# Dynamic convolution and squared-ReLU network: band matrices in one VectorE op, and another order for the softmax pieces and the first loads

## The chip, the cores and the metric

The kernel runs on one core of one Trainium2 chip. The metric is the device time of one execution in microseconds. The kernel before took 760.06 us in the median of eight runs (758.33 to 762.07).

## What is computed

Two stages follow each other. The first is a dynamic convolution over a sequence: each token and each of 8 heads has its own 7 weights, which a softmax makes from `weight_gen`. The second is a feed-forward network with a squared ReLU.

```python
# x: 8 x 4096 x 192, weight_gen: 8 x 4096 x 8 x 7, float32
w = exp(weight_gen - max); w = w / (sum(w) + 1e-9)         # over the 7 taps
x_unf = x_pad[:, s + k, :]                                 # 6 zero rows ahead
out = einsum('bshk,bskhg->bshg', w, x_unf)                 # 24 channels a head
h = np.maximum(out.reshape(32768, 192) @ w_in, 0.0)        # w_in: 192 x 2048
return h * h @ w_out                                       # w_out: 2048 x 192
```

## The kernel before

The 32768 tokens are cut into 64 sub-blocks of 512 tokens, 8 to a batch. `BLOCKS` puts them into 33 blocks: two of one sub-block each, then 31 of two.

**Convolution.** For each sub-block TensorE multiplies pieces of x (tokens on the partitions, 32 channels as the stationary operand) with band matrices. A sub-block has five tiles of 128 tokens that start 104 tokens apart (`STEP`). Each tile gives 104 output columns, the last one 96. A band matrix is the softmax rows of a tile (`wr`, 64 values per token) times a mask that keeps 7 diagonals. `st_band` (L315) makes it on VectorE for one or more tiles in one op, into `bd`. The op is cut as `st_bands` (L474) says: tiles 0 and 1, tiles 2 and 3, tile 4. The first sub-block of a batch has tile 0 alone, because that tile starts at token 0. Where a softmax part ends with the sub-block, tile 4 starts at another place (`tile_start`, L258), and the band has other mask columns. `st_conv` (L372) is the matmuls and the copies of their result to `y` by ScalarE (L401).

**Network.** `st_unit` (L406), called a unit, is six matmuls of 512 columns into one of three PSUM tiles of the pool `ps_h`, which the convolution uses too. ScalarE evicts it with the ReLU into `t` (L424, five buffers). VectorE squares it into `g` (L427). A double block has 16 units, a single one 8. `st_mm2` (L437) is half of the second product for 256 tokens, a quarter of a double block. It runs one block later, into the only pair of output tiles (`ps_o`, one buffer). After the two halves ScalarE copies one of the pair (L461) and VectorE adds the other to it (L462, in `o_sum`). Then the pair is free for the next quarter.

**Order.** The order is written out by hand: the scheduler is set to manual, and each engine executes its instructions in the order in which the program issues them. In `steady`, M is a half of the second product for the block before, u a unit of this block, C the convolution of the next block:

```python
orders = {0: "uuuuuCuuu", 1: "MuMuuuMuuuMCu", 2: "MuuuuMuuuuMuuuuuuuMCu"}
steady = "MuMuuu" * 3 + "MuuuMCu"
```

Ahead of unit u of block j, `run_fill` (L622) issues what the table `fill` holds for (j, u): bands of the next block, exponentials, or a softmax piece (`soft`).

**Softmax.** Each batch is cut into parts (`PARTS`, else one part of 32 rows per partition). Batch 0 has four parts of 8 rows, batch 1 has 8, 8 and 16, batch 2 has 16 and 16. A part has 6 rows of halo and is worked on in pieces of 8 rows (a last piece has 6). A piece is an exponential on ScalarE (L194), and on VectorE a sum (L201), a reciprocal (L208) and the products (L216). Their places are in `TIMES`. The results of small parts go straight into the tiles `wr` by DMAs from SBUF to SBUF (`move_rows`, L491, alternating between the queues of SyncE and GpSimd). Those of large parts are stored in DRAM and read back (`wr_load`).

**Start.** The program loads the first part (s0), w_in and x, computes s0, casts w_in and x on ScalarE (L528, L291), makes the bands and the convolution of sub-block 0, then the exponential, bands and softmax that sub-blocks 1 to 3 need (L536 to L545). GpSimd's queue has the row moves, w_out (L549), a memset of `v_big` (L552) and the x loads of sub-blocks 2 and 3. All loads by GpSimd's queue convert from float32 to float16. The memset at L547 orders the w_out loads behind the cast of x for sub-block 1.

Of the kernel before, what the change touches and what calls it, by code (L numbers as in the profile page):

```python
# [9 lines left out]
def kernel(  # L10
# [25 lines left out]
    nc = tc.nc  # L36
# [10 lines left out]
    P = 128  # L47
# [75 lines left out]
    def cross_w_in(q):  # L123
        for r0, r1 in ((0, RT), (RT, 0)):
            nc.sync.dma_start(out=w_i[r0 : r0 + RT, q, 1], in_=w_i[r1 : r1 + RT, q, 0])
# [132 lines left out]
    def tile_start(j, i):  # L258

        t1 = (j % NBB + 1) * TB  # L260
        return TB - P if i == NT - 1 and t1 in ends(j // NBB) else starts[i]
# [52 lines left out]

    def st_band(j, tiles):  # L315

        if j not in bd_t:
            bd_t[j] = p_bd.tile([P, H * TB], f16, name="bd")
        i = tiles[0]
        lo, hi, n = bounds[i], bounds[tiles[-1] + 1], bounds[i + 1] - bounds[i]  # L320
        shift = 0 if i == 0 and j % NBB == 0 else lo - tile_start(j, i)
        shape = (P, HP * len(tiles), n // SL, 2 * SL)
        nc.vector.tensor_tensor(  # L323
            out=bd_t[j][:, H * lo : H * hi].rearrange(
                "p (g m c) -> p g m c", g=shape[1], c=2 * SL
            ),
            in0=wr_t[j][:, i : tiles[-1] + 1]
            .rearrange("p t g c -> p (t g) c")
            .unsqueeze(2)
            .broadcast_to(shape),  # L330
            in1=mask[:, shift : shift + n]
            .rearrange("p (m c) e -> p m (c e)", c=SL)
            .unsqueeze(1)
            .broadcast_to(shape),
            op=AluOp.mult,
        )
# [35 lines left out]
    def st_conv(j):  # L372

        n = BLOCKS[j][1]
        th = n * TB // 2
        per = 1024 // th
        y = p_y.tile([P, NK, TB], f16, name="y")
        y_t[j] = y
        yps = [
            ps_h.tile([P, 2 * TB], f32, name="yp", tag="h") for _ in range(-(-NK // per))  # L380
        ]
        for later, s, i, q, half, a, b, base in conv_pieces(j):
            lo, hi = bounds[i], bounds[i + 1]
            _, ha, hb, pre = quads[q]
            m, h = (32, hb) if later else (pre, ha)
            bd = bd_t[s][:, H * lo : H * hi].rearrange("p (g c e) -> p g e c", g=HP, e=2)
            p0 = RT * half + 32 * (q % 2)
            k = q // 2
            col = th * (k % per) - base
            nc.tensor.matmul(  # L390
                out=yps[k // per][p0 : p0 + m, col + a : col + b],
                lhsT=x_t[s][:, i, 32 * q : 32 * q + m],
                rhs=bd[:, h // 2, h % 2, a - lo : b - lo],
                start=True,
                stop=True,
                skip_group_check=True,
                tile_position=(0, p0),
            )
        for n, yp in enumerate(yps):
            k0, k1 = n * per, min((n + 1) * per, NK)  # L400
            nc.scalar.copy(  # L401
                out=y[:, k0:k1, 0:th],
                in_=yp[:, 0 : (k1 - k0) * th].rearrange("p (k c) -> p k c", c=th),
            )
# [66 lines left out]
            ],  # L471
        )

    def st_bands(j, part):  # L474

        groups = ((0,), (1,), (2, 3)) if j % NBB == 0 else ((0, 1), (2, 3))
        for tiles in (groups, ((NT - 1,),))[part]:
            st_band(j, tiles)

    with nc.allow_low_precision("fp16 matmul pipeline"), tc.manual_schedule():  # L480

# [42 lines left out]
        s0.total(0, s0.rh)  # L524
        s0.recip(0, s0.rh)
        s0.scale(0, s0.rh, nc.vector)
        for q in (0, 1):
            nc.scalar.copy(out=w_i[:, q, 0], in_=w_st[q])  # L528
        wr_load_sbuf(0, [s0], (0, 2, 1, 4, 3), (nc.sync, nc.gpsimd))
        wr_load_sbuf(1, [s0], range(NT), (nc.gpsimd,))  # L530
        for q in (0, 1):
            cross_w_in(q)
        x_cast(0, nc.scalar.copy)
        x_load_f32(1)
        s1.load(nc.sync)
        for i in (0, 2, 1, 3, 4):  # L536
            st_band(0, (i,))
        st_conv(0)
        s1.exp(0, s1.rh)
        st_bands(1, 0)  # L540
        st_bands(1, 1)
        x_cast(1, nc.vector.tensor_copy)
        s1.total(0, s1.rh)
        s1.recip(0, s1.rh)
        s1.scale(0, s1.rh, nc.vector)  # L545

        nc.gpsimd.memset(x_st[1][:, 0:1], 0.0)  # L547
        for q in range(4):
            load_w_out(q, 4)  # L549
        move_rows(s1)  # L550
        s2.load(nc.sync)
        nc.gpsimd.memset(v_big, 0.0)  # L552
        x_load(2)
        x_load(3)

# [7 lines left out]
        def at(j, u, kind, *args):  # L565
# [2 lines left out]
        PIECE = 8  # L568

        TIMES = {  # L570
            (0, 2): ((1, 7), (2, 1)),
            (0, 3): ((2, 15), (3, 1)),
            (1, 0): ((3, 15), (4, 1)),
            (1, 1): ((4, 15), (5, 1)),
            (1, 2): ((5, 9), (5, 15), (6, 1)),
            (2, 0): ((6, 15), (7, 1), (7, 9)),
            (2, 1): ((8, 1), (8, 15), (9, 1)),
            (3, 0): ((9, 9), (9, 15), (10, 9), (10, 15), (11, 1)),
        }

        EXP_AT = {1: 0, 7: 4, 9: 4, 15: 8}
        loads = {}
        for n, s in enumerate(parts[2:], 2):
            b, f = s.b, s.fb
            k = n - min(m for m, p in enumerate(parts) if p.b == b)
            times = TIMES.get((b, k)) or (
                (f - 6, 15), (f - 5, 15), (f - 4, 15), (f - 3, 9), (f - 3, 15)
            )
            pieces = [(lo, min(lo + PIECE, s.rh)) for lo in range(0, s.rh, PIECE)]
            for (j, u), (lo, hi) in zip(times, pieces, strict=True):  # L590
                at(j, EXP_AT[u], "exp", s, lo, hi)
                at(j, u, "soft", s, lo, hi)
            if n > 2:
                loads.setdefault(times[0][0] - 1, []).append(s)
        for j in range(1, NBLK - 1):
            a = BLOCKS[j + 1][0]
            when = (1, 9, 5, 9)
            if j == 1:
                when = (1, 1, 3, 3)
            elif j == 2:  # L600
                when = (5, 6, 8, 9)
            elif j in (3, 4, 5):
                when = (5, 7, 9, 11)
            elif j == 6:
                when = (9, 9, 11, 11)
            for u, args in zip(when, ((a, 0), (a, 1), (a + 1, 0), (a + 1, 1))):
                at(j, u, "band", *args)

        stored, waiting = set(), []

# [11 lines left out]
        def run_fill(j, u):  # L622
            for kind, *args in fill.get((j, u), ()):
                if kind == "band":
                    st_bands(*args)
                    continue
                s, lo, hi = args
                if kind == "exp":
                    s.exp(lo, hi)
                    continue  # L630
                s.total(lo, hi)
                s.recip(lo, hi)
                s.scale(lo, hi, nc.vector)
                if hi < s.rh:
                    continue
                if s.r == FIRST:
                    move_rows(s)
                    after = parts[parts.index(s) + 1]
                    if after.b == s.b and after.r > FIRST:
                        s.store(nc.sync)  # L640
                else:
                    s.store(nc.sync)
                    stored.add(s)
                    for w in [w for w in waiting if w[0] is s]:
                        waiting.remove(w)
                        load_rows(w[1])

        FCS = (range(NF // 2), range(NF // 2, NF))
        for j, (sub, n) in enumerate(BLOCKS):
            for s in loads.get(j, ()):  # L650
                s.load(nc.sync)
            if j + 2 < NBLK:
                load_rows(j + 2)
            u = m = 0
            for step in orders.get(j, steady):
                if step == "M":
                    qt, part = divmod(m, 2)
                    m += 1
                    if part == 0:
                        o = new_o(ps_o, None)  # L660
                    st_mm2(j - 1, qt, FCS[part], (0, 1), o)
                    if part == 1:
                        o_sum(j - 1, qt, (0, 1), o)
                        if qt % 2:
                            o_store(j - 1, qt - 1, range(4), nc.sync)
                elif step == "u":
                    run_fill(j, u)
                    st_unit(j, u)
                    u += 1
                elif j + 1 < NBLK:  # L670
                    st_conv(j + 1)
            if 0 < j < NBLK - 2:
                for k in range(BLOCKS[j + 2][0], sum(BLOCKS[j + 2])):
                    x_load(k)

# [46 lines left out]
```

The softmax here doesn't subtract the row's maximum and nothing guards it: scores larger than these inputs give would overflow.

## Time and profile before

| | before |
|---|---|
| median of eight runs, us | 760.06 |
| profiled execution, us | 761.96 |
| its span, us | 760.0 |
| mean granted TensorE clock | 0.991 |
| TensorE busy, us (matmuls) | 742.2 (15266) |
| VectorE busy, us (instructions) | 630.7 (1119) |
| ScalarE busy, us (instructions) | 623.6 (753) |
| band ops on VectorE (L323) | 201, 157.9 us |

All rows but the first are of one profiled execution, which is 1.9 us above the median. Its time is 2.0 us longer than its span, the time from the first instruction to the end of the last one. Busy time is the time in which an engine had an instruction in execution. In rows of groups, the numbers after the bar are busy time, the mean of one in ns, and the idle time of the engine just ahead of them with what ended it. In rows of waits the numbers are microseconds in total, how many times, and the longest. In rows of the timeline they are start and length in microseconds, and in brackets the idle time before. PE is TensorE, DVE VectorE, ACT ScalarE, POOL GpSimd, SP SyncE.

### The profile page before, as it was taken

Reading aid. Unit: us, or ns where it says so; the run is one execution under the profiler, and the core shown is the slowest. Engines: PE = TensorE matmul, PEld = TensorE weight load, DVE = VectorE, ACT = ScalarE, POOL = GpSimd, SP = SyncE. Lnnn points to the kernel's source line nnn. Section 1 sums busy time; section 2 is a strip of 40 time slices with the busy share of each in tenths; the row PEclk is TensorE's granted clock in tenths of the full one; section 3 lists DMA queues with packets and bytes.
Section 4 is the critical chain, followed back from the end, with each engine's and each line's share of the span. In section 5 each row is a group of like instructions: output and inputs, shape, how many; then the busy total and the mean of one; then the engine's idle time right before and its main releaser. Section 6 shows DMA issues by size and latency. Waiting matters only on the chain.

```text
span 760.0 us, 33723 instructions
## 1 busy us (share of the span) xinstructions
PE 742.2 (98%) x15266; PEld 560.1 (74%) x15266; DVE 630.7 (83%) x1119; ACT 623.6 (82%) x753; POOL 87.3 (11%) x126
## 2 busy tenths in 40 slices
PE   7899999999999999999999999999999999999998
PEld 4757877877787777777777777777777777777777
DVE  5888999898899988898888888888888887778853
ACT  3887889878888888888888888888888888888883
POOL 3522212011100110010100110001100011000000
PEclk8899999999999999999999999999999999999999
DMA  7844532546325544344445323454422454332311
GB/s 227 121 80 84 102 89 60 101 103 138 70 59 123 107 78 59 101 79 85 80 77 117 89 64 56 78 134 89 78 60 42 79 107 76 60 68 49 56 45 64
DMA packets 122395, 65.23 MB, mean 86 GB/s; under 512 B 83881, under 2 KB 118668, under 8 KB 121740
## 3 DMA queue, kind: packets, MB, share of 16 engines
q1 hardware_dynamic: 78012, 46.46, 21.4%
q0 software_dynamic: 44096, 16.53, 19.7%
q8 instruction: 119, 1.95, 1.0%
q14 instruction: 24, 0.20, 0.1%
q10 hardware_dynamic: 144, 0.10, 0.0%
HBM read 48.61 MB, written 28.70 MB: 102 GB/s over the span
## 4 chain that ended last, share of the span: by engine, by line
PE 86%; DVE 5%; issue 2%; DMA 1%; ACT 1%; POOL 0%; POOLq 0%; SPq 0%; DVEq 0%
PE o L447 42%; PE h L415 39%; PE yp L390 5%; DVE g L427 2%; DVE bd L323 2%; DMA xt<-in_x_dram 1%; DVE o_sb L462 1%; ACT o_sb L461 0%; DMA wr<-v_first 0%; ACT t L424 0%; DVE v_big L216 0%; DVE rcp L208 0%; DVE ssum L201 0%; POOL xt L277 0%; POOL xt L271 0%
## 5 line engine op out<-in xcount | busy, mean ns | idle before, releaser
L424 ACT ACTIVATE t<-h 128x1024 f16<-128x1024 f32 x512 | 496.9, 1027 | 71.2 <-PE h L415 69.5
L427 DVE TENSOR_TENSOR g<-t 128x1024 f16<-128x1024 f16 x512 | 336.3, 686 | 97.9 <-ACT t L424 95.8
L447 PEld LDWEIGHTS <-g 64*128 64x128 f16 x8192 | 351.1, 94 | 61.2 <-issue 8.9
L447 PE MATMUL o<-w_o,g 64*128 64x192 f16 x8192 | 384.2, 243 | 5.7 <-DVE o_sb L462 4.7
L415 PE MATMUL h<-y,w_i 64*128 64x512 f16 (+1 forms) x3168 | 380.3, 373 | 4.2 <-ACT t L424 2.7
L415 PEld LDWEIGHTS <-w_i 64*128 64x128 f16 x3168 | 164.0, 95 | 118.2 <-issue 6.5
L323 DVE TENSOR_TENSOR bd<-wr,mask 128x1664 f16<-128x1664 f16 (+2 forms) x201 | 157.9, 829 | 4.9 <-DMA wr<-v_first 4.9
L277 POOL DMA_DIRECT2D xt<-in_x_dram x62 | 51.3, 832 | 442.9 <-PE yp L390 420.0
L461 ACT COPY o_sb<-o 128x384 f32<-128x384 f32 x129 | 62.2, 482 | 33.5 <-PE o L447 33.5
L462 DVE TENSOR_TENSOR o_sb<-o,o_sb 128x384 f32<-128x384 f32 x129 | 71.1, 551 | 13.0 <-ACT o_sb L461 7.1
L401 ACT CAST y<-yp 128x1024 f16<-128x1024 f32 (+1 forms) x64 | 48.2, 803 | 15.9 <-PE yp L390 15.8
L390 PE MATMUL yp<-bd,xt 128*32 128x104 f16 (+8 forms) x3864 | 52.0, 209 | 3.1 <-ACT xt L291 1.8
L390 PEld LDWEIGHTS <-xt 128*32 128x32 f16 (+3 forms) x3864 | 46.2, 92 | 9.3 <-issue 6.0
L194 ACT ACTIVATE ex<-wg 128x448 f32<-128x448 f32 (+2 forms) x44 | 27.2, 618 | 6.5 <-DMA wg<-in_weight_gen_dram 6.5
L201 DVE TENSOR_REDUCE ssum<-ex 128x64 f32<-128x448 f32 (+2 forms) x44 | 26.1, 592 | 3.7 <-ACT ex L194 3.7
L216 DVE TENSOR_TENSOR v_big<-ex,rcp 128x112 f16<-128x112 f32 (+1 forms) x136 | 27.3, 263 | 1.2
L208 DVE RECIPROCAL rcp<-ssum 128x64 f32<-128x64 f32 (+2 forms) x44 | 23.7, 539 | 1.5
L307 POOL DMA_DIRECT2D wr<-v_first x31 | 16.8, 562 | 27.2 <-DVE v_first L216 27.2
L267 POOL DMA_DIRECT2D xt<-in_x_dram x7 | 3.8, 549 | 137.5 <-PE yp L390 137.5
L508 PE MATMUL wp<-warm 128*128 128x512 f16 x42 | 11.0, 430 | 1.3 <-DVE warm L500 1.3
L508 PEld LDWEIGHTS <-warm 128*128 128x128 f16 x42 | 4.5, 109 | 7.3 <-issue 2.4
L216 DVE TENSOR_TENSOR v_first<-ex,rcp 128x112 f16<-128x112 f32 (+1 forms) x48 | 9.1, 255 | 0.3
(17 smaller groups left out, 23.9 us busy)
## 6 DMA issues: line engine op xcount, KB each, us to landing
out_dram<-o_sb SPq DMA_DIRECT2D x63, 384.0 KB, 2.6
xt<-in_x_dram POOLq DMA_DIRECT2D x42, 240.0 KB, 5.9
wg<-in_weight_gen_dram SPq DMA_DIRECT2D x4, 1064.0 KB, 6.5
xt<-in_x_dram POOLq DMA_DIRECT2D x20, 192.0 KB, 6.3
wr<-vd SPq DMA_DIRECT2D x38, 80.0 KB, 5.0
vd<-v_big SPq DMA_DIRECT2D x5, 512.0 KB, 5.7
wg<-in_weight_gen_dram SPq DMA_DIRECT2D x6, 392.0 KB, 4.7
wg<-in_weight_gen_dram SPq DMA_DIRECT2D x3, 616.0 KB, 6.1
```

The source lines that it names most:

```text
L194: nc.scalar.activation(out=self.ex[:, lo:hi].rearrange("p r g k e -> p (r g) k e"), in_=self.wg[:, lo:hi].rearrange("p r (g e) k -> p (r g ...
L216: eng.tensor_tensor(out=bass.AP(tensor=v.tensor, offset=v.offset + lo * H * SL + lo % SL * 2 + g * SL * 2, ap=[list(v.ap[0]), [H * SL + 2, ...
L277: eng.dma_start(out=dst[:, first:last], in_=ap)
L323: nc.vector.tensor_tensor(out=bd_t[j][:, H * lo : H * hi].rearrange("p (g m c) -> p g m c", g=shape[1], c=2 * SL), in0=wr_t[j][:, i : tile ...
L390: nc.tensor.matmul(out=yps[k // per][p0 : p0 + m, col + a : col + b], lhsT=x_t[s][:, i, 32 * q : 32 * q + m], rhs=bd[:, h // 2, h % 2, a - ...
L401: nc.scalar.copy(out=y[:, k0:k1, 0:th], in_=yp[:, 0 : (k1 - k0) * th].rearrange("p (k c) -> p k c", c=th),)
L415: nc.tensor.matmul(out=h[:, half, jj * th : (jj + 1) * th], lhsT=w_in_chunk(u * per + jj, slot, half), rhs=y_t[j][r0 : r0 + RT, k, 0:th], ...
L424: nc.scalar.activation(out=t1, in_=h, func=ActF.Relu)
L427: nc.vector.tensor_tensor(out=g, in0=t1, in1=t1, op=AluOp.mult)
L447: nc.tensor.matmul(out=oo[:, cc * Dm : (cc + 1) * Dm], lhsT=g[r0 : r0 + RT, cc * P : (cc + 1) * P], rhs=w_o[r0 : r0 + RT, fc, :], start=(f ...
L461: nc.scalar.copy(out=o_sb, in_=o[0][:, c])
L462: nc.vector.tensor_tensor(out=o_sb, in0=o[1][:, c], in1=o_sb, op=AluOp.add)
```

## The change

It has four parts.

1. All five band tiles have the same width of 104 columns, the last one included, so that `bd` has 520 columns per head and not 512. `st_bands` makes one op of all five tiles. Tile 0 stays alone at the start of a batch, and tile 4 stays alone where a softmax part ends. The convolution reads the same columns as before.
2. The second softmax part, s1, is worked on within block 0: its exponential ahead of unit 4, the rest ahead of unit 5.
3. The softmax pieces get new places in `TIMES`. A place (j, 0) is the first unit of a block, with the exponential ahead of unit 12 (unit 5 for j = 2) of the block before. The bands of the next block are issued at two units, not at up to four. Loads of `weight_gen` are issued at unit 0, after the row loads.
4. The first loads have another order. The cast of x comes between the two casts of w_in, and the load of the second x comes ahead of the second pair of copies within w_in. Of w_out, two quarters wait for the convolution of sub-block 0 (a memset into its x tile) and two for the cast of the second x. The third part's `weight_gen` comes by GpSimd's queue, ahead of the memset of `v_big`. The x loads of sub-blocks 2 and 3 are issued after block 0.

```diff
     def st_band(j, tiles):
+
         if j not in bd_t:
-            bd_t[j] = p_bd.tile([P, H * TB], f16, name="bd")
+            bd_t[j] = p_bd.tile([P, H * NT * STEP], f16, name="bd")
         i = tiles[0]
-        lo, hi, n = bounds[i], bounds[tiles[-1] + 1], bounds[i + 1] - bounds[i]
+        lo = STEP * i
         shift = 0 if i == 0 and j % NBB == 0 else lo - tile_start(j, i)
+        n = min(STEP, P - shift)
         shape = (P, HP * len(tiles), n // SL, 2 * SL)
         nc.vector.tensor_tensor(
-            out=bd_t[j][:, H * lo : H * hi].rearrange(
+            out=bd_t[j][:, H * lo : H * (lo + len(tiles) * n)].rearrange(
...
-            lo, hi = bounds[i], bounds[i + 1]
+            lo = bounds[i]
+            hi = lo + (STEP if tile_start(s, i) == starts[i] else bounds[i + 1] - lo)
...
-    def st_bands(j, part):
-
-        groups = ((0,), (1,), (2, 3)) if j % NBB == 0 else ((0, 1), (2, 3))
-        for tiles in (groups, ((NT - 1,),))[part]:
-            st_band(j, tiles)
+    def st_bands(j):
+        first = int(j % NBB == 0)
+        last = NT - int(tile_start(j, NT - 1) != starts[-1])
+        for tiles in (range(first), range(first, last), range(last, NT)):
+            if tiles:
+                st_band(j, tiles)
...
-        for q in (0, 1):
-            nc.scalar.copy(out=w_i[:, q, 0], in_=w_st[q])
+        nc.scalar.copy(out=w_i[:, 0, 0], in_=w_st[0])
         wr_load_sbuf(0, [s0], (0, 2, 1, 4, 3), (nc.sync, nc.gpsimd))
         wr_load_sbuf(1, [s0], range(NT), (nc.gpsimd,))
-        for q in (0, 1):
-            cross_w_in(q)
+        cross_w_in(0)
         x_cast(0, nc.scalar.copy)
         x_load_f32(1)
+        nc.scalar.copy(out=w_i[:, 1, 0], in_=w_st[1])
+        cross_w_in(1)
         s1.load(nc.sync)
         for i in (0, 2, 1, 3, 4):
             st_band(0, (i,))
         st_conv(0)
-        s1.exp(0, s1.rh)
-        st_bands(1, 0)
-        st_bands(1, 1)
+        st_bands(1)
         x_cast(1, nc.vector.tensor_copy)
-        s1.total(0, s1.rh)
-        s1.recip(0, s1.rh)
-        s1.scale(0, s1.rh, nc.vector)
-
+
+        nc.gpsimd.memset(x_t[0][:, 0, 0:1], 0.0)
+        for q in (0, 1):
+            load_w_out(q, 4)
         nc.gpsimd.memset(x_st[1][:, 0:1], 0.0)
-        for q in range(4):
+        for q in (2, 3):
             load_w_out(q, 4)
-        move_rows(s1)
-        s2.load(nc.sync)
+        s2.load(nc.gpsimd)
         nc.gpsimd.memset(v_big, 0.0)
-        x_load(2)
-        x_load(3)
...
-            (0, 2): ((1, 7), (2, 1)),
-            (0, 3): ((2, 15), (3, 1)),
-            (1, 0): ((3, 15), (4, 1)),
-            (1, 1): ((4, 15), (5, 1)),
-            (1, 2): ((5, 9), (5, 15), (6, 1)),
-            (2, 0): ((6, 15), (7, 1), (7, 9)),
-            (2, 1): ((8, 1), (8, 15), (9, 1)),
-            (3, 0): ((9, 9), (9, 15), (10, 9), (10, 15), (11, 1)),
+            (0, 2): ((1, 7), (2, 0)),
+            (0, 3): ((2, 15), (3, 0)),
+            (1, 0): ((3, 15), (4, 0)),
+            (1, 1): ((4, 15), (5, 0)),
+            (1, 2): ((4, 1), (5, 1), (5, 15)),
+            (2, 0): ((6, 1), (6, 15), (7, 0)),
+            (2, 1): ((7, 9), (7, 15), (8, 15)),
+            (3, 0): ((9, 9), (9, 15), (10, 9), (10, 15), (11, 0)),
...
-        EXP_AT = {1: 0, 7: 4, 9: 4, 15: 8}
+        def exp_time(j, u):
+
+            if u == 0:
+                return j - 1, 5 if j == 2 else 12
+            return j, {1: 0, 7: 3, 9: 4, 15: 8}[u]
+
+        at(0, 4, "exp", s1, 0, s1.rh)
+        at(0, 5, "soft", s1, 0, s1.rh)
...
-            when = (1, 9, 5, 9)
-            if j == 1:
-                when = (1, 1, 3, 3)
-            elif j == 2:
-                when = (5, 6, 8, 9)
-            elif j in (3, 4, 5):
-                when = (5, 7, 9, 11)
-            elif j == 6:
-                when = (9, 9, 11, 11)
-            for u, args in zip(when, ((a, 0), (a, 1), (a + 1, 0), (a + 1, 1))):
-                at(j, u, "band", *args)
+            small = [p for p in parts if p.fb <= j + 1][-1].r == FIRST
+            us = {1: (1, 3), 2: (6, 8), 6: (7, 9)}.get(j, (5, 9) if small else (1, 5))
+            for n, u in enumerate(us):
+                at(j, u, "band", a + n)
...
-            if 0 < j < NBLK - 2:
+            if j == 0:
+                x_load(2)
+                x_load(3)
+            elif j < NBLK - 2:
                 for k in range(BLOCKS[j + 2][0], sum(BLOCKS[j + 2])):
                     x_load(k)
```

## The prediction

> **What bounds the kernel now.** I read the busy totals first, then TensorE's waits, then the timelines of the stretches where it waits.
>
> ```profile
> PE 742.2 (98%) x15266; PEld 560.1 (74%) x15266; DVE 630.7 (83%) x1119; ACT 623.6 (82%) x753; POOL 87.3 (11%) x126
> PEclk8899999999999999999999999999999999999999
> ```
>
> TensorE sets the time. Its stream (15,266 matmuls, in one order) is the same in both kernels, so only waits and the clock can change. I cut the trace at the copies that empty each convolution (L401), one place per block. Undisturbed double blocks take 22.54 us (676 to 701 us into the span, for instance). Everything above that is loss: block 0 takes 11.1 us and block 2 takes 20.4, blocks 3, 6, 7, 8, 9 and 11 take 25.36, 23.77, 24.25, 23.47, 23.59 and 23.07. From block 12 on there are two small excesses, without a VectorE wait. Block 6, for instance, lies between these two rows of the timeline:
>
> ```profile
> 130.66 1.50 ACT L401 CAST y<-yp 128x1024 f16<-128x1024 f32 x2 [0.52 <-PE yp L390]
> 154.42 1.50 ACT L401 CAST y<-yp 128x1024 f16<-128x1024 f32 x2 [0.76 <-PE yp L390]
> ```
>
> What TensorE waits for, first from 12.2 to 62.4 us, then from 85 to 280 us:
>
> ```profile
> PE h L415 <- ACT t L424: 2.7, 2, 2.4
> PE yp L390 <- ACT xt L291: 1.8, 1, 1.8
> PE o L447 <- DVE o_sb L462: 1.5, 1, 1.5
> ```
>
> ```profile
> PE o L447 <- DVE o_sb L462: 3.2, 6, 0.7
> PE o L447 <- issue: 0.3, 1, 0.3
> ```
>
> In the middle the wait is always the same: the next quarter of the second product needs the one pair of output banks, which VectorE frees with its addition (L462), and VectorE is late. Its timeline shows why (block 7):
>
> ```profile
> 160.27 0.56 DVE L462 TENSOR_TENSOR o_sb<-o,o_sb 128x384 f32<-128x384 f32 x1
> 160.74 0.61 DVE L201 TENSOR_REDUCE ssum<-ex 128x64 f32<-128x448 f32 x1
> ...
> 162.72 1.95 DVE L323 TENSOR_TENSOR bd<-wr,mask 128x1664 f16<-128x1664 f16 x2
> 164.59 2.49 DVE L427 TENSOR_TENSOR g<-t 128x1024 f16<-128x1024 f16 x4
> 167.00 0.55 DVE L462 TENSOR_TENSOR o_sb<-o,o_sb 128x384 f32<-128x384 f32 x1
> ```
>
> A quarter lasts 5.2 us on TensorE (two halves of 1.32, four units of 0.65). VectorE has 0.5 + 4 x 0.6 = 2.9 us of fixed work in it. A softmax piece (2.0) and a pair of bands (1.9) make 6.8: too much for one quarter, though the block as a whole has room.
>
> The start, from the whole timeline:
>
> ```profile
> 20.44 0.94 ACT L194 ACTIVATE ex<-wg 128x784 f32<-128x784 f32 x1 [4.56 <-DMA wg<-in_weight_gen_dram]
> 21.28 4.86 ACT L424 ACTIVATE t<-h 128x1024 f16<-128x1024 f32 x5
> 22.34 2.74 PE L415 MATMUL h<-y,w_i 64*128 64x256 f16 x24 [2.38 <-ACT t L424]
> ...
> 32.45 2.42 DVE L323 TENSOR_TENSOR bd<-wr,mask 128x1664 f16<-128x1664 f16 x3
> ...
> 40.74 0.55 DVE L462 TENSOR_TENSOR o_sb<-o,o_sb 128x384 f32<-128x384 f32 x1
> ...
> 62.29 2.17 PE L447 MATMUL o<-w_o,g 64*128 64x192 f16 x31 [1.48 <-DVE o_sb L462]
> ```
>
> ScalarE stands 4.56 us before the second part's exponential with block 0's evictions behind it; later, up to 62 us, VectorE is the limit.
>
> [...]
>
> **Part 1: bands in one op.** Rows of the groups by shape:
>
> ```profile
> L323 DVE TENSOR_TENSOR bd<-wr,mask 128x1664 f16<-128x1664 f16 x119 | 116.3, 1016 | 1.4 <-DMA wr<-v_first 1.4
> L323 DVE TENSOR_TENSOR bd<-wr,mask 128x768 f16<-128x768 f16 x64 | 33.1, 549 | 0.0
> ```
>
> Slope (1016 - 549) / 896 = 0.521 ns per element, fixed part 549 - 400 = 149 ns. So 4160 elements take 2.32 us and 3328 take 1.88. Ops of a row overlap by about 0.07, so three (2.42 us measured for 1664, 1664, 768) become 2.25: 0.17 us less per sub-block. There are 89 band ops in place of 201, some 11 us of VectorE time in all. From block 12 on VectorE is not waited for, so this is worth 0 there; if it became the bound, 0.35 per block. The op is longer than any part before, but it stands right behind the addition (units 1 and 5): 0.5 + 2.25 + 2.4 = 5.15 us in a quarter of 5.2. It fits, barely. Matmul count and columns stay; the padded eight columns are never read.
>
> **Part 2: pieces and bands spread.** Blocks 3 to 6 get bands at units 5 and 9 (or 7 and 9) in place of up to 11, later blocks at 1 and 5, never 9. Softmax pieces of unit 1 go to unit 0, ahead of the square of unit 0, after the end-of-block slack (convolution 1.6 and one unit 0.65, in which VectorE owes nothing). I replayed the heaviest boundaries with T the end of the last half. Block 6 to 7: addition done T+1.9 at worst, piece 2.0, square, piece 1.65, square, addition at about T+7.0; TensorE needs it at 2.25 + 1.32 + 0.65 + 1.32 + 1.95 = T+7.5. Block 4 to 5 has a third piece at unit 1: its next addition comes at about T+12.2 against T+12.65. So the quarter of 6.8 us is gone everywhere, with 0.1 to 0.5 us to spare. Worth: the excess of blocks 6 to 11 is 1.23 + 1.71 + 0.93 + 1.05 + 0.53 = 5.45 us; less 0.34 of an "issue" gap in block 9, and 0.7 for slips where the slack is thin: **4.4 us**. Bounds 2 and 5.4. One load can be late: block 7's rows now are wanted at unit 7 of block 6, but the part before them ends about 4 us earlier, so they come in time within 1 us.
>
> **Part 3: the start.** The cast of x goes ahead of the second w_in cast, so the first convolution waits for its bands instead (11.89 plus five at 0.51, 14.5): copy at 14.9, not 15.08, 0.2 us. The second x load, formerly held by that cast (issued 14.35), goes out near 11.6, ahead of two of the w_in crossings. GpSimd's queue does a tiny memset after convolution 0, then w_out in two pairs (from 15, not 20.75), the third part's load, the 2.5 us memset of v_big, and only then the row moves and the x loads of sub-blocks 2 and 3.
> Block 0 now: units at half clock 1.34 each (36 matmuls in 4.03 us), evictions free to run: the fourth ends 21.95, the exponential 22.8, the fifth eviction 23.75, units 5 to 7 and the convolution by 25.2 (before 28.1). But VectorE takes the second softmax (3.34 us, 21.41 to 24.75 before) after the fifth square, 24.4 to 27.75: **three us later**. Squares 5 to 7 follow until 29.6, and the second half ends at 30.0 (before 31.4). The row moves start at 27.75; taking 1.9 us of issues and 2.9 of landing, the rows of sub-block 2 are there at 32.4 (31.5 with an empty queue, 34.5 at the 4.4 us of before). VectorE, free at 31.1, waits 1.3 with four squares behind it; bands, squares and addition then end at 41.2, against 41.29. x of sub-block 3 is there by 38 to 39, the convolution done by 40.1. So up to 41 us nothing is gained: the load wait moved to the rows. **0 us**, bounds -1.5 and +2.
> Block 2: pieces at (1,7) and (2,0) run back to back, so the idle 1.02 (squares waiting for ScalarE) and 0.88 (rows) on VectorE go, and two band pairs save 0.34, 2.2 in all; followed square by square, 0.4 of it comes back as waits for evictions. The addition that ended at 62.25 ends near 60.5: **1.8 us**. In block 3 the half-clock stretch (3.4 us, costs 1.7) may or may not recur, since about 1 us of wait remains there: half of it, **0.8 us**, less 0.3 for the two pieces at that boundary.
>
> **Sum**, against the profiled execution's own 761.96 us (span 760.0): 4.4 + 0 + 1.8 + 0.5 = 6.7 us. That execution is 1.9 above the median of the eight; the difference carries over: 760.06 - 6.7 = **753.4**.
>
> **Rivals.**
> A (0.55): as summed, 753.4, own range 751.5 to 755.
> B (0.20): the middle gains, the start gives nothing, because the rows land at 34 us or the clock drops anyway. 760.06 - 4.4 + 0.5 = 756.2. For it: the thin replay. Against: two VectorE idle stretches do go.
> C (0.10): the crowding only moves to the block boundaries; two adjacent pieces of 3.65 us delay the addition and the six waits return with new places. 759.5. For it: margins of 0.1 to 0.5 us. Against: 2.25 us without a due addition at each boundary.
> [...]
> [...]
> That the ops don't merge is excluded: the built program has 42 of 4160 elements.
>
> **How the numbers follow.** The eight runs span 758.33 to 762.07; 0.2%, 1.5 us, is about what can be told from no change. Faster: A, B, E and a little of C, 0.83. Same: most of C, 0.08. Slower: D, 0.09. The range leaves out D, half of C and the far end of E: 750.3 to 758.8.
>
> **What would show it.** TensorE's waits for the addition between 85 and 280 us: under 0.7 us in total, not 3.2. Blocks 6 to 9 at 22.6 to 22.8. The 4160 row near 2.32 us. ScalarE's 4.56 us gone; VectorE waiting 0.5 to 2.5 us for v_first rows near 31; the addition that ended at 62.25 ending near 60.5. Wrong if that row wait exceeds 4 us, if new waits for the addition stand at block starts 5, 6, 7, or if half clock covers more than the 13.6 us it does now.

## The result and the profile after

The changed kernel takes 753.69 us in the median of 11 runs (752.71 to 756.10); the kernel before took 759.94 in 31. The ratio is 0.9916 with a 95% interval of 0.9907 to 0.9926, that is 6.4 us less (5.6 to 7.1). The forecast was 753.4, in a range of 750.3 to 758.8. One of its steps had the wrong sign all the same, as the experiments show.

The profiled execution took 754.03 us with a span of 751.8. Its page, busy totals and clock:

```profile
PE 738.8 (98%) x15266; PEld 565.5 (75%) x15266; DVE 624.2 (83%) x1007; ACT 623.3 (83%) x753; POOL 88.0 (12%) x128
PEclk9999999999999999999999999999999999999999
```

VectorE has 112 instructions fewer and is busy for 6.5 us less. The granted clock of TensorE was 1.00 up to 745 us (0.89 from there on). Before, it stood at 0.50 twice near the start, from 15.2 to 25.2 us and from 63.0 to 66.0. The two largest band rows by shape:

```profile
L325 DVE TENSOR_TENSOR bd<-wr,mask 128x4160 f16<-128x4160 f16 x42 | 97.2, 2315 | 2.2 <-DMA wr<-v_first 2.2
L325 DVE TENSOR_TENSOR bd<-wr,mask 128x3328 f16<-128x3328 f16 x21 | 39.5, 1882 | 0.1
```

The lengths are those of the forecast (2.32 and 1.88 us). The idle time ahead of them is 2.2 us, all of it for the moved softmax rows.

Between 85 and 280 us the table of TensorE's waits is empty. It had 3.2 us for VectorE's addition, which frees the output pair. Block 6 lies between these two copies of the timeline and takes 23.16 us, not 23.77; block 7 takes 22.56, not 24.25:

```profile
127.34 1.50 ACT L404 CAST y<-yp 128x1024 f16<-128x1024 f32 x2 [0.44 <-PE yp L393]
150.50 1.50 ACT L404 CAST y<-yp 128x1024 f16<-128x1024 f32 x2 [0.44 <-PE yp L393]
```

Blocks 6 to 11 together are 0.75 us over six undisturbed ones of 22.54, not 5.44. VectorE's timeline over the second and third quarter of block 6:

```profile
137.96 0.55 DVE L465 TENSOR_TENSOR o_sb<-o,o_sb 128x384 f32<-128x384 f32 x1
...
140.62 2.32 DVE L325 TENSOR_TENSOR bd<-wr,mask 128x4160 f16<-128x4160 f16 x1
142.86 1.28 DVE L430 TENSOR_TENSOR g<-t 128x1024 f16<-128x1024 f16 x2
144.06 0.55 DVE L465 TENSOR_TENSOR o_sb<-o,o_sb 128x384 f32<-128x384 f32 x1
144.53 2.31 DVE L325 TENSOR_TENSOR bd<-wr,mask 128x4160 f16<-128x4160 f16 x1
```

One band op stands in a quarter, and no softmax piece beside it; the additions come in time, but for 0.13 us at the second.

The start, the three largest of TensorE's waits from 12.2 to 62.4 us:

```profile
PE yp L393 <- DMA xt<-in_x_dram: 2.0, 1, 2.0
PE o L450 <- DVE o_sb L465: 1.5, 2, 1.2
PE h L418 <- ACT t L427: 1.4, 2, 1.3
```

and the timeline of the same stretch:

```profile
20.98 0.94 ACT L194 ACTIVATE ex<-wg 128x784 f32<-128x784 f32 x1 [0.68 <-DMA wg<-in_weight_gen_dram]
...
31.87 2.32 DVE L325 TENSOR_TENSOR bd<-wr,mask 128x4160 f16<-128x4160 f16 x1 [1.60 <-DMA wr<-v_first]
...
37.85 1.59 PE L393 MATMUL yp<-bd,xt 128*32 128x104 f16 x118 [1.96 <-DMA xt<-in_x_dram]
...
39.99 0.55 DVE L465 TENSOR_TENSOR o_sb<-o,o_sb 128x384 f32<-128x384 f32 x1
...
60.65 1.48 PE L450 MATMUL o<-w_o,g 64*128 64x192 f16 x31 [1.16 <-DVE o_sb L465]
```

ScalarE's wait of 4.56 us is down to 0.68. In its place VectorE waits 1.60 for rows, and TensorE 1.96 for x. By 60.65 us the kernel is 1.64 ahead (before: 62.29). Block 3 then takes 23.44 us, not 25.36. The kernel before had its second stretch at a clock of 0.50 there; in this execution the clock is 1.00 from 62.3 to 85.5 us.

### The profile page after: what moved, and what is told of

Same layout as the page of the kernel before. It is cut to its first block, busy times and chain, and to the rows that moved or that the text cites. A ratio compares the mean times of both kernels' runs of the same rounds, so it can differ in the third digit from the quotient of the medians.

```text
span 751.8 us, 33616 instructions
## 1 busy us (share of the span) xinstructions
PE 738.8 (98%) x15266; PEld 565.5 (75%) x15266; DVE 624.2 (83%) x1007; ACT 623.3 (83%) x753; POOL 88.0 (12%) x128
## 4 chain that ended last, share of the span: by engine, by line
PE 88%; DVE 5%; DMA 3%; issue 1%; SPq 1%; ACT 1%; POOL 0%; DVEq 0%; ACTq 0%
PE o L450 42%; PE h L418 40%; PE yp L393 6%; DVE g L430 2%; DVE bd L325 1%; DMA wr<-v_first 1%; DMA wg<-in_weight_gen_dram 1%; DMA w_st<-in_moe_w_in_dram 1%; DMA vd<-v_big 1%; ACT t L427 1%; DVE v_first L216 0%; DVE o_sb L465 0%; DVE rcp L208 0%; DVE ssum L201 0%; POOL wr L307 0%
## 5 line engine op out<-in xcount | busy, mean ns | idle before, releaser
L450 PEld LDWEIGHTS <-g 64*128 64x128 f16 x8192 | 354.9, 94 | 54.5 <-issue 3.5
L418 PEld LDWEIGHTS <-w_i 64*128 64x128 f16 x3168 | 169.9, 94 | 111.8 <-issue 5.3
L325 DVE TENSOR_TENSOR bd<-wr,mask 128x4160 f16<-128x4160 f16 (+3 forms) x89 | 149.4, 1701 | 5.8 <-DMA wr<-v_first 5.7
```

The lines of the kernel that those rows point to most:

```text
L325: nc.vector.tensor_tensor(out=bd_t[j][:, H * lo : H * (lo + len(tiles) * n)].rearrange("p (g m c) -> p g m c", g=shape[1], c=2 * SL), in0= ...
L418: nc.tensor.matmul(out=h[:, half, jj * th : (jj + 1) * th], lhsT=w_in_chunk(u * per + jj, slot, half), rhs=y_t[j][r0 : r0 + RT, k, 0:th], ...
L450: nc.tensor.matmul(out=oo[:, cc * Dm : (cc + 1) * Dm], lhsT=g[r0 : r0 + RT, cc * P : (cc + 1) * P], rhs=w_o[r0 : r0 + RT, fc, :], start=(f ...
```

## Experiments

Three theories were open: the spreading of VectorE's work makes the gain (mine), the merged op makes it, or the start with its clock. The first four kernels ran on one chip, beside 43 executions of the kernel before at 760.51 us. Each kernel has one profile, of one of its executions. "Block 3 begins" means the copy that empties its convolution.

**1. The merged op alone.**

```diff
-        st_bands(1, 0)
-        st_bands(1, 1)
+        st_bands(1)
...
-            for u, args in zip(when, ((a, 0), (a, 1), (a + 1, 0), (a + 1, 1))):
-                at(j, u, "band", *args)
+            for n, u in enumerate((when[0], when[2])):
+                at(j, u, "band", a + n)
```

(`st_band`, `st_bands` and the columns of the convolution are those of the changed kernel. The merged op stands where the first of the three ops stood, so tile 4 also moves to an earlier unit in most blocks.)

> Part 1 alone: one band op of five tiles per sub-block, issued where the kernel before issued its first band op of that sub-block; softmax pieces and start as before. Theory (spreading of VectorE's work makes the gain, merging gives only 0.17 us of VectorE per sub-block and takes the last tile off units 9 to 11): 757 to 759 us, with some waits of TensorE for the addition left between 85 and 280 us (1 to 2.5 us of the 3.2). Rival 'the merged op makes the gain': 754 to 755, waits gone. Rival 'an op of 2.3 us blocks the squares': 761 or more.

Measured: 761.68 us, ratio 1.0016 (1.0009 to 1.0023): slower by 1.2 us. My figure was wrong in sign; the result is that of the third outcome, that the long op blocks the squares. TensorE's waits between 85 and 280 us in this kernel, and then VectorE's wait for rows from 16 to 62 us:

```profile
PE o L450 <- DVE o_sb L465: 4.5, 6, 1.1
```

```profile
DVE bd L325 <- DMA wr<-v_first: 2.0, 2, 1.9
```

The additions are later than before (3.2 us). And VectorE waits 2.0 us for rows, where it waited 0.9: the merged op reads the rows of all five tiles. In the two profiles block 2 is 1.1 us longer, and blocks 6 to 11 are 6.29 us over, not 5.44. As tile 4 moved too, this run alone doesn't tell the joining from the place; experiments 4 and 10 do.

**2. The new places alone**, with three band ops per sub-block, issued together.

```diff
+    def st_bands(j):
+        groups = ((0,), (1,), (2, 3), (NT - 1,)) if j % NBB == 0 else ((0, 1), (2, 3), (NT - 1,))
+        for tiles in groups:
+            st_band(j, tiles)
```

(`TIMES`, the exponentials, the units of the bands and the loads at unit 0 are those of the changed kernel; the start is that of the kernel before.)

> Part 3 alone: the new places of pieces, bands and weight_gen loads, with the bands still in three ops each (two, two and one tile) at one place; start as before. Theory: 755 to 756.5 us, the waits for the addition between 85 and 280 us under 1 us, blocks 6 to 9 at 22.6 to 22.8 us. Rival 'merging makes it': 758.5 or more. Rival 'the start makes it': 759 or more.

Measured: 755.31 us, ratio 0.9929 (0.9911 to 0.9947), 5.4 us less. The waits for the addition between 85 and 280 us:

```profile
PE o L447 <- issue: 0.3, 1, 0.3
PE o L447 <- DVE o_sb L462: 0.2, 1, 0.2
```

0.2 us is left of 3.2, with not one merged op. The new places alone do it. Block 6 still takes 23.48 us, more than the 22.6 to 22.8 that I had expected. Which of the places counts most (bands, pieces, exponentials or loads) was not separated.

**3. The start alone** (parts 2 and 4, bands and later pieces as before).

```diff
-        s1.exp(0, s1.rh)
         st_bands(1, 0)
         st_bands(1, 1)
         x_cast(1, nc.vector.tensor_copy)
-        s1.total(0, s1.rh)
-        s1.recip(0, s1.rh)
-        s1.scale(0, s1.rh, nc.vector)
...
+        at(0, 4, "exp", s1, 0, s1.rh)
+        at(0, 5, "soft", s1, 0, s1.rh)
```

(with the loads of the changed kernel's start)

> Parts 2 and 4 alone: the new order of the first loads and the second softmax part inside block 0; bands and later pieces as before. Theory: 757.5 to 759 us (the start gains 1 to 2.5 us, the six waits in the middle stay at about 3.2 us). Rival 'the start makes the gain, by the TensorE clock that no longer falls to half': 754 to 755.5.

Measured: 759.30 us, ratio 0.9983 (0.9973 to 0.9992): 1.3 us less, inside the gain that I forecast, though the time lies just above its range. The six waits in the middle are unchanged at 3.2 us. The clock is not the whole of it: five executions of this kernel with a mean clock of 1.000 took 757.6 to 758.7, far from 754.

**4. The changed kernel with three band ops.**

```diff
-        for tiles in (range(first), range(first, last), range(last, NT)):
-            if tiles:
-                st_band(j, tiles)
+        for tiles in groups:
+            st_band(j, tiles)
```

(with the groups of experiment 2, and 512 columns per head)

> The changed kernel with the bands in three ops each (four at the start of a batch) at the new places. Theory: 0.3 to 1.5 us over the changed kernel (754 to 755.2), all of it before 85 us, where VectorE is the limit. Rival 'merging makes the gain': 757 or more. Rival 'the long op costs something': under 753.5.

Measured: 752.27 us, ratio 0.9892 (0.9874 to 0.9910), against 0.9916 (0.9907 to 0.9926) of the changed kernel. By the figure it is the third outcome, which I had not believed: the merge costs something here too. The two intervals still touch, so it was run again below. The table of VectorE's waits from 16 to 62 us has no row for the moved rows. Block 3 begins at 57.98 us, not 58.80, and from there on the blocks agree but for short gaps of TensorE that come at other places in each execution.

The next four kernels ran on another chip, where 11 executions of the kernel before took 760.67.

**5. Three ops in the first six sub-blocks, merged ones later.**

```diff
-        for tiles in (range(first), range(first, last), range(last, NT)):
+        cuts = (range(first), range(first, last), range(last, NT))
+        if j < 6:
+            cuts = (range(first), range(first, 2), range(2, 4), range(4, NT))
+        for tiles in cuts:
```

> The changed kernel, but sub-blocks 0 to 5 get their bands in ops of two, two and one tile at the same units; all later sub-blocks keep the merged op. Theory M (the merged op waits for the rows of all five tiles, which are moved by separate DMAs, 1.60 and 0.65 us in the changed kernel's trace at 31.9 and 50.1 us, where VectorE is the limit): 751.8 to 752.9 us, as with three ops everywhere, and no wait for v_first rows over 0.3 us after 20 us. Rival 'a 2.3 us op is bad anywhere': 753.3 or more.

Measured: 753.70 us, ratio 0.9919 (0.9903 to 0.9935). By the figure this is the changed kernel's time, and the rival's ("bad anywhere"), so theory M failed by its own test. The trace says half of it: the row waits are gone, and the addition of 39.99 us comes at 38.35. But x landed late, and TensorE stood:

```profile
35.51 0.23 PE L393 MATMUL yp<-bd,xt 128*32 128x104 f16 x2
38.47 2.74 PE L393 MATMUL yp<-bd,xt 128*32 128x104 f16 x118 [2.73 <-DVE g L430]
```

The row puts the wait down to a square. The x load issued at 31.05 landed at 38.42, and the matmuls began at 38.47, so x is the likely cause. They took 2.74 us and not 1.59; why is not shown. This execution took 756.39, though, 2.7 over the median of its own kernel, so it can't speak for the others. Against the rival speak four other profiles. From the start of block 3 to the end they take 693.0 and 693.1 us with the merged op (the changed kernel and experiment 9), and 692.4 and 694.0 with three ops (experiments 4 and 10). No cost of the long op shows there.

**6. x ahead of the row moves.**

```diff
                 elif j + 1 < NBLK:
                     st_conv(j + 1)
+                    if j == 0:
+                        x_load(2)
+                        x_load(3)
...
-            if j == 0:
-                x_load(2)
-                x_load(3)
-            elif j < NBLK - 2:
+            if 0 < j < NBLK - 2:
```

> The changed kernel with the x loads of sub-blocks 2 and 3 issued right after the convolution of sub-block 1, ahead of the row moves in GpSimd's queue. TensorE's longest wait, 1.96 us for x at 37.9, should go. Theory (the wait is covered: VectorE's addition ends at 40.5 in any case): 753.2 to 754.0 us, no change. Rival 'the longest wait is on the path': 751.7 to 752.3.

Measured: 755.11 us, ratio 0.9931 (0.9918 to 0.9945), no gain. The x loads landed by 29.82 us, and the wait for x is gone; one of 1.37 us for the bands stands in its place, behind the same wait of VectorE for rows (1.60 us). So TensorE's longest wait was covered by VectorE. The figure lies 1.1 us above the forecast; against the changed kernel the intervals overlap. A cause is not shown; in this profile the copies within w_in were late (waits of 1.23 and 1.70 us at 19 to 21 us), at a point that the edit doesn't reach.

**7. The second softmax part one unit earlier on VectorE.**

```diff
-        at(0, 5, "soft", s1, 0, s1.rh)
+        at(0, 4, "soft", s1, 0, s1.rh)
```

> The changed kernel with the second softmax part's VectorE work ahead of the square of unit 4 in block 0 instead of behind it. VectorE stood idle 1.75 us ahead of that square, so the piece and the row moves come about 1.5 us earlier. Theory (up to 62 us VectorE and the rows set the time): 752.0 to 753.0. Rival 'the order of two works on one engine changes nothing': 753.4 to 754.0.

Measured: 751.05 us, ratio 0.9887 (0.9870 to 0.9904), some 2.2 us better than the changed kernel by the two ratios, more than expected. One line of program code does it. In VectorE's timeline the first merged op has no wait (it had 1.60):

```profile
30.28 0.56 DVE L465 TENSOR_TENSOR o_sb<-o,o_sb 128x384 f32<-128x384 f32 x1
30.75 2.32 DVE L325 TENSOR_TENSOR bd<-wr,mask 128x4160 f16<-128x4160 f16 x1
```

What makes the gain is less clear. This is the slowest of the five executions (753.67), and its copies within w_in were late: TensorE waits 2.8 us for them, against 0.4 in the changed kernel's first profile and 2.2 in that of experiment 9. So its row moves start at 26.80 us, no earlier than in the first (26.83) and 1.2 earlier than in the other (27.96). They landed after 2.0 us in the median, not 3.0.

**8. Part 2 undone.**

```diff
         st_conv(0)
+        s1.exp(0, s1.rh)
         st_bands(1)
         x_cast(1, nc.vector.tensor_copy)
+        s1.total(0, s1.rh)
+        s1.recip(0, s1.rh)
+        s1.scale(0, s1.rh, nc.vector)
...
+        move_rows(s1)
         s2.load(nc.gpsimd)
...
-        at(0, 4, "exp", s1, 0, s1.rh)
-        at(0, 5, "soft", s1, 0, s1.rh)
```

> The changed kernel with part 2 undone: the second softmax part ahead of block 0, as before, its row moves too. Theory (ScalarE waits again for that load, 2 us or more, with the evictions of block 0 behind it, and VectorE has less to do meanwhile): 754.7 to 756. Rival 'the order of the loads makes the start's gain, part 2 nothing': 753.3 to 754.2. Rival 'the earlier rows outweigh it': under 753.

Measured: 756.28 us, ratio 0.9946 (0.9931 to 0.9961), 2.3 us worse than the changed kernel by the ratios and just above the forecast. TensorE waits for ScalarE's evictions again:

```profile
23.26 2.75 PE L418 MATMUL h<-y,w_i 64*128 64x256 f16 x24 [3.86 <-ACT t L427]
```

The clock is lower again too: all six executions have a mean of 0.992 to 0.995, where the changed kernel's eleven have 0.995 to 1.000. Part 2 is worth having; experiment 7 shows that its place was not the best.

The last four ran later on the chip of experiments 5 to 8, beside 10 new executions of the kernel before, which took 761.50.

**9 and 10. The changed kernel again, and again with three ops.** The code is that of the changed kernel and of experiment 4.

> The changed kernel again, unaltered, as the measure for the next three on the same chip. Expected 753.2 to 754.2 us, 0.990 to 0.993 of the kernel before.

> The changed kernel with three band ops per sub-block everywhere, again. Theory M (the merged op costs 1 to 2 us, as it waits for five tiles' rows and holds VectorE longer): 751.8 to 752.8 us, at least 0.7 below the unaltered changed kernel. Rival 'the first figure was chance, the merge costs nothing where the pieces are spread': within 0.5 us of it.

Measured: 754.69 us, ratio 0.9908 (0.9890 to 0.9926), and 753.18 us, ratio 0.9895 (0.9877 to 0.9914). Both lie 0.4 to 0.5 us above the times expected. Three ops are 1.5 us better by the medians and 1.0 by the ratios; in experiment 4 it was 1.8 by the ratios. Each pair of intervals overlaps; the two agree in sign, and so do the places where block 3 begins: 58.80 and 59.52 with the merged op, 57.98 and 57.86 with three. The two largest of VectorE's waits from 16 to 62 us, first with the merged op, then with three:

```profile
DVE g L430 <- ACT t L427: 3.0, 2, 2.7
DVE bd L325 <- DMA wr<-v_first: 2.7, 3, 1.3
```

```profile
DVE g L427 <- ACT t L424: 2.9, 2, 2.7
DVE xt L291 <- DMA x_st<-in_x_dram: 2.1, 1, 2.1
```

**11. Three ops, the softmax part at unit 4, x early**: the edits of experiments 4, 7 and 6 together.

> Three band ops per sub-block, the second softmax part's VectorE work ahead of the square of unit 4, and the x loads of sub-blocks 2 and 3 ahead of the row moves. Theory (VectorE, rows and x are three limits one behind the other at 30 to 40 us, each alone gains little): 749.5 to 751 us. Rival 'they do not add up': 751 to 752, as the softmax move alone.

Measured: 753.06 us, ratio 0.9889 (0.9870 to 0.9908). That is the ratio of experiment 7 alone, so as times go they don't add up, and both forecasts were too low. In the profile block 3 begins at 56.67 us, 1.2 earlier than in experiment 7, yet the medians don't show it; the profile of experiment 7 is of its slowest execution.

**12. The same with w_out later.**

```diff
-        nc.gpsimd.memset(x_t[0][:, 0, 0:1], 0.0)
-        for q in (0, 1):
-            load_w_out(q, 4)
         nc.gpsimd.memset(x_st[1][:, 0:1], 0.0)
-        for q in (2, 3):
+        for q in range(4):
             load_w_out(q, 4)
```

> As the one before, with all four w_out loads behind the cast of the second x (about 18 us), not two of them from 13.9 us on. In the changed kernel's trace the second copies within w_in take 5.4 us to land and the second part's weight_gen 6.7, against 2.7 and 4.9 in the kernel before. Theory (w_out takes the queues from them): crossing back under 4 us, weight_gen landed by 19.5, 748.5 to 750. Rival 'w_out comes too late for the first second-product': over the one before.

Measured: 751.89 us, ratio 0.9872 (0.9852 to 0.9892), the lowest ratio of all and 2.8 us below the changed kernel of experiment 9. It misses the forecast of 748.5 to 750, and its interval overlaps that of experiment 11, so the 1.2 us between the two are not clear of noise. Block 3 begins at 55.92 us. The reason that I gave is only half right. DMA issues from 10 to 20 us, with size and median time to landing, in the changed kernel and then here:

```profile
w_i<-w_i SPq DMA_DIRECT2D x4, 192.0 KB, 4.1
wg<-in_weight_gen_dram SPq DMA_DIRECT2D x1, 392.0 KB, 6.7
```

```profile
w_i<-w_i SPq DMA_DIRECT2D x4, 192.0 KB, 4.2
wg<-in_weight_gen_dram SPq DMA_DIRECT2D x1, 392.0 KB, 5.8
```

`weight_gen` lands sooner without w_out (14.4 + 5.8 = 20.2 us, not 20.9), though not by 19.5. The copies within w_in take as long as before: the second pair took 5.7 us here and 5.4 there. So w_out isn't what delays them. What stands right ahead of them on SyncE's queue in both is the second x load; in the kernel before, where they went first, they took 2.7. The first pair, issued ahead of that load, takes 2.7 here too. That it is this order was not tried.

## Why the prediction was right, and where it was wrong

**Part 2 (the middle): right.** 4.4 us forecast; the excess of blocks 6 to 11 fell from 5.44 to 0.75, by 4.7. Experiment 2 shows that the places alone take it to 1.10. The thin margins nearly held: one wait for the addition is left in the trace, of 0.13 us, in block 6.

**Part 1 (the merge): wrong in sign.** The op's length was exact, but two steps failed. The first is the saving, "0.17 us less per sub-block". The overlap of 0.07 us with the next op was taken off the merged op and not off the three. From the start of the bands to that of the next op it is 2.33 us with three ops (experiment 4) and 2.24 with one: 0.09 us. VectorE's busy time fell by 6.5 us in all, not by some 11. The second is "VectorE, free at 31.1, waits 1.3 with four squares behind it; ... the load wait moved to the rows". The wait came (1.60), but the prediction charged it to the later softmax part alone and put the merge's share at nothing. The first of three ops needs the rows of two tiles, the merged op those of all five, which ten DMAs for two sub-blocks bring, issued some 0.6 us apart on each of two queues. With three ops at the same places no such wait is left (experiments 4, 5 and 10).

Alone, the merge with its earlier tile 4 costs 1.2 us; undone in the changed kernel, it gives 1.0 to 1.8 by the ratios, with overlapping intervals. The traces show two places of cost: the rows (1.60 + 0.65 us of idle VectorE in the changed kernel) and, where pieces crowd, the quarter (4.5 us of waits in experiment 1 for 3.2). How the loss in the changed kernel arises stays open, since experiment 5 took the row waits away and gained nothing measurable.

**Part 3 (the start): right in sum.** Up to 41 us 0 was forecast; the addition ended at 40.5, not 41.3, in the first profile, and TensorE went on at 41.4 in that of experiment 9. The 4.56 us wait went, and the rows took its place, as forecast. For the landing of the row moves 2.9 us were put in: in the trace of before the ten from 24 to 30 us took 4.5 in the median (4.3 to 5.0), and in that of the changed kernel 3.0 (1.8 to 4.4). The x loads were put at 38 to 39 us, and came at 37.8. For block 2 1.8 us were forecast: TensorE went on at 60.65, not 62.29, so 1.6 us, and in the profile of experiment 9 0.9. Alone the start is worth 1.3 us, but undoing part 2 in the changed kernel costs 2.3.

**The clock: a size.** The prediction counts 13.6 us of half clock in the kernel before, 3.4 of them in block 3. The trace has the clock at 0.50 from 15.2 to 25.2 us and from 63.0 to 66.0, and at 0.52 in the mean from 62.8 to 66.2; with the edges that is about the figure. Half of 1.7 us was forecast for block 3; it gave 1.9 in this profile. How much of it belongs to the change is open. With the new places block 3 takes 23.4 to 23.5 us in every profile, and the clock is 1.00 from 62.3 to 85.5 us in those of the changed kernel and of experiments 2 and 9. But experiment 1, with the places and the start of before, takes 23.37 us too; before and in experiment 3 it is 25.36. In these two a wait of 1.5 us stands near the start of the block; the wait at the same place is 1.2 us or less in every other profile. That the clock in block 3 hangs on this wait was not tried.

At the start the change does count. In the 98 executions with a clock on record that work s1 ahead of block 0 (the kernel before, experiments 1, 2 and 8), the mean clock never exceeds 0.998. In the 74 that work it within block 0, it is 0.999 or 1.000 in 39. That goes with part 2: experiment 8 has all the rest of the change. Waits need not be gone for it: in the profile of experiment 9 the clock is 1.00 from 13.9 to 24.2 us (0.56 before), with 2.2 us of waits for w_in. Rival E (0.06) had a better clock at the start and about 3 us more from it, 750.5. The clock came, at 1.00 over the same stretch in the profile of the changed kernel; the 3 us did not. The profile suggests why: up to 62 us VectorE and the loads set the pace, not TensorE.

**From the profile to the median: luck.** "The difference carries over" was off. Of 43 executions of the kernel before, 9 had a mean clock of 0.990 to 0.993 and took 761.5 us in the median; the other 34 took 760.3. The profile that I read was of that kind (0.991). Two errors of like size cancelled. Between the two profiled executions the spans differ by 8.2 us, where the sum said 6.7; most of the rest is block 3 (1.9 us less, where 0.8 was put in). But their times (7.9 us apart) differ by 1.7 us more than the medians (6.25 apart). That 753.4 came so near 753.69 is luck; that the middle makes most of the gain is not.

**The rivals.** C, crowding at the block boundaries, is excluded by the empty table of waits. D (0.09), slower at 762.3 with late rows and one more stretch of half clock, didn't come: in the first profile rows landed by 34 us and the clock was 1.00 up to 745. B, no gain in the start, is excluded by experiment 3.

## What to carry to other kernels

Read an engine's load per deadline, not per kernel: VectorE was at 83% and late six times, because a softmax piece and a pair of bands, both movable, stood between the same two additions. The new places gave 5.4 us, with no work removed. Before joining small ops into one, look at what each waits for. The joined op here waited for the rows of all five tiles and held VectorE for 2.3 us, and the 0.09 us that it saved did not pay for that. And check whether the profile in hand is a typical execution before carrying its difference over to the median.

## What was not expected of the hardware

- The second pair of copies within SBUF took 2.7 to 3.0 us to land where it went ahead of the second x load (the kernel before, experiments 1 and 2), and 4.9 to 7.0 right behind this 384 KB load on the same queue (all other kernels). That the load is the cause was not tried.
- The TensorE clock of one program differs between executions: the kernel before had a mean granted clock from 0.990 to 0.998 in 43 executions, and a second stretch at a clock of 0.50 (63.0 to 66.0 us) in the profiled one, where block 3 took 25.36 us and not 23.44 as in the changed kernel's.
- The same x load (192 KB as it lands), issued between 31.0 and 31.8 us, landed after 5.1 to 7.4 us in the profiles of different kernels, enough to decide which wait was last.
